# Second layer's output product by Strassen's scheme, as a phase of its own, and one written order for the first layer

## The chip, the cores and the metric

The kernel runs on one core of one Trainium2 chip. The metric is the device time of one execution in microseconds (us), lower is better. One execution was also profiled; rows below are from that one.

## What is computed

Three stages follow each other (reference, cut):

```python
# q, k, v: (4, 8, 576, 64), phi: (4, 8, 576, 32)
a = softmax(phi, axis=seq)                    # pools 576 keys into 32
k_m, v_m = a.T @ k, a.T @ v                   # per batch and head
x = softmax(q @ k_m.T / 8) @ v_m              # -> x: (2304, 512)
h = max(x @ w1, x @ w2, x @ w3)               # first layer, 512 -> 768
y = h @ w_out                                 # 768 -> 512
h2 = y @ w_in                                 # second layer, 512 -> 2048
g = max(h2, 0) + log1p(exp(-abs(h2)))         # softplus
out = g @ w_out2                              # 2048 -> 512
```

The feed-forward weights arrive as 64-bit floats, seen as pairs of 32-bit words. Products of large matrices are made in three fp32r matmuls from split operands: each operand is written as a high part (rounded to fp32r) plus the rest, and hi*hi, lo*hi and hi*lo are added up in PSUM.

## The kernel before, in words

*First layer.* Attention runs in 8 units (batch b, group g of four heads). A list PLAN, walked inside a manual schedule, gives the order of all five engines by steps: loads (ph, ld, q, wl), pooling (mx, ex, ax, tr), transposes of q (qT), scores and softmax (sc, s0, s1, s2, fin), weight conversion (ca, c7, wo), the products U = v_m * w (u, u6), x * w as U times attention (m1), splits of h (hs) and y = h * w_out (mo, ev). PLAN covers the first half of the tokens (1152 of 2304). The second half is done after it by phase_a (L743: m1 for six column blocks j, with conversions and U of later blocks put in by slots) and phase_o (L772: m1out and the evictions y_out, L717). There the order on each engine is left to the scheduler, which takes what its own timing model holds ready. y0_split (L853) splits the first half's y into y0h and y0l, one of twelve pieces in each of slots 4 to 15 of phase_a.

*Second layer.* The 2048 inner columns f come in 16 blocks of 128, four at a time (fg), the tokens in 6 chunks ck of 384: 96 steps (fg, ck, fi). In a step, m2in (L878) makes h2 for a block and chunk with 12 matmuls of 384 columns (4 blocks of dm x 3 split products) into one of two pst banks. soft1 (L894) takes |h| on VectorE (L896), softplus(-|h|) on ScalarE (L898) and max(h, 0) + that on VectorE (L900). soft2 (L903) splits it: gh by a cast on ScalarE, gl by a subtraction on GpSimd (both by the helpers cast, L189, and rest, L197). m2out (L942) multiplies by the output weights: 3 token tiles x 3 split products, 9 matmuls of 512 columns into three acc banks that add up over the four fi. After each (fg, ck) the sums are added to O in SBUF (L974), after the last fg stored. m2out of a step is two steps behind its m2in. Two m2in steps are done inside phase_o.

*Weights of the second layer.* w2_load (L836) loads a block of w_in and w_out2 (512 KB each); Conv.a joins the two 32-bit words to fp32 (top on ScalarE, then L234, L235, L238 on VectorE), Conv.b casts on ScalarE and subtracts on GpSimd. w2_steps (L847) hangs load, a and b on step numbers.

Engines work in the order of their own queues. A tile pool gives each tag a fixed number of buffers (bufs); a new tile of the tag waits until all uses of an older one have ended. The second layer's order is the scheduler's, with program order as priority.

Of the kernel before, what the change touches and what calls it, by code (L numbers as in the profile page):

```python
# [111 lines left out]
@with_exitstack
def fused_kernel(ctx: ExitStack, tc: tile.TileContext, q, k, v, phi, w1, w2, w3, w_out, m_in, m_out, out):
# [318 lines left out]
    def att_q(u):  # L432
# [30 lines left out]
        for s in range(3):  # L463
            ev(s, qps[s])
            if s < 2:
                yield
# [559 lines left out]
```

## Time and profile before

| what | value |
|---|---|
| timed runs | 714.68, 714.69, 710.29 us; median 714.68 |
| profiled execution | 711.26 us, span 709.5 us, mean granted clock 0.987 |
| TensorE matmul busy | 672.6 us (95%) in 4216 matmuls |
| VectorE / ScalarE / GpSimd busy | 415.6 / 302.9 / 258.2 us |
| HBM read / written | 53.74 / 4.72 MB |

The span goes from the first to the last instruction; the 1.8 us between it and the profiled time lie around it. PE is the TensorE matmul, PEld its weight load, DVE VectorE, ACT ScalarE, POOL GpSimd, SP SyncE, which issues the DMAs. Matmuls overlap, so the duration of one is longer than its distance to the next: what a matmul costs is read from the chain (time of a row by its count).

### The profile page before, as it was taken

To read this page: it belongs to the slowest core of one execution; us is meant where nothing else is said; L and a number is where in the kernel's file an instruction comes from. 1 tells how busy PE (TensorE), PEld (TensorE's weight loads), DVE (VectorE), ACT (ScalarE), POOL (GpSimd) and SP (SyncE) were. 2 spreads that over 40 slices of the span, in tenths; PEclk is the share of its full clock that TensorE was granted. 3 is DMA by queue.
4 is the path that set the end of the run, shared out by engine and by line. 5 is a ranking of instruction groups with operands and counts; after the bars stand their busy time and mean duration, and the time that the engine had idled before them with its cause. 6 is when DMAs were issued, how large, how long until landed. Compare 5 with 4: busy or idle time off the path is not lost.

```text
span 709.5 us, 11378 instructions
## 1 busy us (share of the span) xinstructions
PE 672.6 (95%) x4216; PEld 602.5 (85%) x4216; DVE 415.6 (59%) x785; ACT 302.9 (43%) x644; POOL 258.2 (36%) x278
## 2 busy tenths in 40 slices
...
GB/s 228 273 287 122 269 270 132 221 30 90 60 140 100 1 1 149 118 90 1 1 0 1 106 131 1 1 0 33 117 89 1 1 1 0 1 46 45 45 45 89
DMA packets 57463, 59.19 MB, mean 83 GB/s; under 512 B 9792, under 2 KB 52288, under 8 KB 57408
## 3 DMA queue, kind: packets, MB, share of 16 engines
...
q14 instruction: 22, 0.18, 0.1%
HBM read 53.74 MB, written 4.72 MB: 82 GB/s over the span
## 4 chain that ended last, share of the span: by engine, by line
PE 76%; DMA 8%; DVE 7%; ACT 3%; issue 2%; POOL 2%; SPq 1%; DVEq 0%; ACTq 0%; POOLq 0%
PE acc L953 28%; PE pst L890 28%; PE psm L661 11%; DMA kvm<-in_v_dram 2%; PE psm L711 2%; PE psm L712 2%; PE psm L713 2%; DMA kvm<-in_k_dram 2%; SPq L166 1%; DVE cg L235 1%; PE psm L607 1%; DMA qr<-in_q_dram 1%; DMA qn<-in_q_dram 1%; POOL y0l L199 1%; DMA pre<-in_q_dram 1%
## 5 line engine op out<-in xcount | busy, mean ns | idle before, releaser
L199 POOL TENSOR_TENSOR gl<-m,gh 128x384 fp32r<-128x384 f32 x96 | 100.2, 1044 | 241.5 <-ACT gh L191 233.9
L896 DVE TENSOR_SCALAR e<-pst 128x384 int32<-128x384 int32 x96 | 53.4, 556 | 147.9 <-PE pst L890 147.9
L898 ACT ACTIVATE L<-e 128x384 f32<-128x384 f32 x96 | 50.3, 524 | 183.8 <-DVE e L896 183.8
L953 PE MATMUL acc<-ol,gh 128*128 128x512 f32 x288 | 113.4, 394 | 0.0
L953 PE MATMUL acc<-oh,gh 128*128 128x512 f32 x288 | 113.3, 394 | 0.0
L890 PE MATMUL pst<-yb,ih 128*128 128x384 f32 x384 | 106.2, 337 | 0.0
L661 PE MATMUL psm<-ah,uh 128*128 128x288 f32 x288 | 87.4, 305 | 5.1 <-ACT mt L668 3.1
L900 DVE SCALAR_TENSOR_TENSOR m<-pst,L 128x384 f32<-128x384 f32 x96 | 53.5, 557 | 59.7 <-ACT L L898 59.7
L661 PE MATMUL psm<-al,uh 128*128 128x288 f32 x288 | 85.0, 295 | 1.2 <-DVE al L199 1.2
L661 PE MATMUL psm<-ah,ul 128*128 128x288 f32 x288 | 84.8, 295 | 0.0
L953 PE MATMUL acc<-oh,gl 128*128 128x512 f32 x288 | 81.9, 392 | 0.0
L191 ACT ACTIVATE gh<-m 128x384 fp32r<-128x384 f32 x96 | 50.3, 524 | 57.7 <-DVE m L900 57.5
L890 PEld LDWEIGHTS pst<-yb,ih 128*128 128x128 f32 x384 | 70.2, 188 | 2.2
L890 PE MATMUL pst<-y0l,ih 128*128 128x384 f32 x192 | 64.8, 337 | 0.0
L953 PEld LDWEIGHTS acc<-oh,gl 128*128 128x128 f32 x288 | 54.1, 188 | 12.5
L890 PE MATMUL pst<-y0h,ih 128*128 128x384 f32 x192 | 64.6, 337 | 0.0
L890 PE MATMUL pst<-yb,il 128*128 128x384 f32 x192 | 64.5, 336 | 0.0
L890 PE MATMUL pst<-y0h,il 128*128 128x384 f32 x192 | 64.5, 336 | 0.0
L661 PEld LDWEIGHTS psm<-ah,uh 128*128 128x128 f32 x288 | 54.2, 189 | 9.3 <-ACT mt L668 4.1
L953 PEld LDWEIGHTS acc<-oh,gh 128*128 128x128 f32 x288 | 53.9, 187 | 8.8 <-DVE yb L199 0.2
L953 PEld LDWEIGHTS acc<-ol,gh 128*128 128x128 f32 x288 | 54.1, 188 | 8.3
L661 PEld LDWEIGHTS psm<-al,uh 128*128 128x128 f32 x288 | 54.2, 188 | 1.4 <-DVE al L199 1.4
...
## 6 DMA issues: line engine op xcount, KB each, us to landing
wraw<-in_moe_w_dram SPq DMA_DIRECT2D x66, 256.0 KB, 4.1
raw<-in_moe_w_in_dram SPq DMA_DIRECT2D x16, 512.0 KB, 3.6
raw<-in_moe_w_out_dram SPq DMA_DIRECT2D x16, 512.0 KB, 3.5
kvm<-in_k_dram SPq DMA_DIRECT2D x8, 512.0 KB, 6.6
kvm<-in_v_dram SPq DMA_DIRECT2D x8, 512.0 KB, 5.8
wor<-in_moe_w_out_dram SPq DMA_DIRECT2D x6, 512.0 KB, 3.7
ph<-in_phi_dram SPq DMA_DIRECT2D x8, 256.0 KB, 4.1
qn<-in_q_dram SPq DMA_DIRECT2D x4, 512.0 KB, 6.0
```

The costliest lines, as they stand in the source:

```text
L166: eng.dma_start(**kw)
L191: nc.scalar.activation(out=dst, in_=src, func=AF.Copy)
L199: return e.tensor_tensor(out=dst, in0=src, in1=hi, op=ALU.subtract)
L661: nc.tensor.matmul(x, l[:, t, ws], r[:, cs], start=(n == 0), stop=(n == 5))
L711: nc.tensor.matmul(x, wh[:, ds], hi, start=first, stop=False)
L712: nc.tensor.matmul(x, wl[:, ds], hi, start=False, stop=False)
L713: nc.tensor.matmul(x, wh[:, ds], lo, start=False, stop=last)
L890: i = nc.tensor.matmul(hx, l[:, ds], r[:, cs], start=(n == 0), stop=(n == 3 * ND - 1))
L896: nc.vector.tensor_scalar(out=e.bitcast(I32), in0=hx.bitcast(I32), scalar1=0x7FFFFFFF, scalar2=None, op0=ALU.bitwise_and)
L898: nc.scalar.activation(out=L, in_=e, func=AF.Softplus, scale=-1.0)
L900: nc.vector.scalar_tensor_tensor(out=m, in0=hx, scalar=0.0, in1=L, op0=ALU.max, op1=ALU.add)
L953: nc.tensor.matmul(acc[0][t], l[:, t * P:(t + 1) * P], r, **kw)
```

## The change

1. m2in, soft and the order (fg, ck, fi) of the 96 steps stay, but a step's softplus result isn't split and multiplied: it is written to DRAM (Gd) in m. FORD makes the blocks of both inner halves alternate, so that the first inner quarter of both halves is complete after two fg. PSUM for m2in: six psx banks.
2. After the 96 steps comes the output product by Strassen's scheme (in the form with 7 products and shared sums). The tokens' halves (tile t and t + 9), the inner halves and the halves of the 512 output columns make the 2 x 2 blocks. 18 units (t, kh) each load four 128x512 tiles (g_load), form sums and split seven operands (g_parts), and multiply (g_mm: 7 operands x 4 blocks j x 3 split products of 256 columns). After both kh of a tile, g_out combines the seven products and stores two tiles.
3. The output weights are loaded and joined by pairs (w2_raw, q_join), combined (q_sums) and split (q_parts), spread over the steps; the last two pairs after the loop. Their split parts for pairs 4 to 7 go into the memory of y0, ya and yb.
4. PLAN is new and covers the whole first layer, with all of its second half, the splits of y (y0, ev2), the conversion of the first four w_in blocks (w2c) and the first three m2in steps; phase_a and phase_o go. att_q evicts a transposed block before the third is made. The fence on DMAs after PLAN (LOADED) goes.

```diff
@@ second layer: one step
-        G[n] = m
-    def soft2(n):
-        m = G[n]
-        gh = s_p.tile([P, CH], F32R, tag="gh", name="gh", bufs=3)
-        gl = s_p.tile([P, CH], F32R, tag="gl", name="gl", bufs=3)
-        cast("act", gh, m)
-        rest("pool", gl, m, gh)
-        G[n] = (gh, gl)
+        m = late["s"].tile([P, CH], F32, tag="m", name="m", bufs=4)
+        nc.vector.scalar_tensor_tensor(out=m, in0=hx, scalar=0.0, in1=e, op0=ALU.max, op1=ALU.add)
+        yield
+        half, i = divmod(FORD[fg * FG + fi], NP)
+        kh, j = divmod(i, FG)
+        if (ck, half, kh) not in Gd:
+            Gd[ck, half, kh] = gd_p.tile([NTT, P, FG, P], F32, name=f"gd{ck}{half}{kh}")
+        dma(out=Gd[ck, half, kh][:, :, j].rearrange("t p c -> p t c"), in_=m.rearrange("p (t c) -> p t c", t=NTT))
...
+    def x_tile():
+        return g_p.tile([P, DM], F32, tag="x", name="x", bufs=6)
...
+    def q_sums(i):
+        g1, g2 = J[2 * i], J[2 * i + 1]
+        WQ[i] = wq_tiles(i)
+        ta, tb = TS[i] = [x_tile() for _ in range(2)]
+        t1, t2, t4, t3 = ta[:, 0:Q], ta[:, Q:], tb[:, 0:Q], tb[:, Q:]
+        e = nc.gpsimd if i < FG + 2 else nc.vector
+        e.tensor_tensor(out=t1, in0=g1[:, Q:], in1=g1[:, 0:Q], op=ALU.subtract)
+        e.tensor_tensor(out=t2, in0=g2[:, Q:], in1=t1, op=ALU.subtract)
+        e.tensor_tensor(out=t4, in0=t2, in1=g2[:, 0:Q], op=ALU.subtract)
+        e.tensor_tensor(out=t3, in0=g2[:, Q:], in1=g1[:, Q:], op=ALU.subtract)
+    def q_parts(i):
...
+        for k, (h, l, x) in enumerate(((h0[:, 0:Q], l0[:, 0:Q], g1[:, 0:Q]), (h0[:, Q:3 * Q], l0[:, Q:3 * Q], g2),
+                                       (h0[:, 3 * Q:], l0[:, 3 * Q:], ta[:, 0:Q]), (h1[:, 0:Q], l1[:, 0:Q], ta[:, Q:]),
+                                       (h1[:, Q:], l1[:, Q:], tb))):
+            cast("act", h, x)
+            rest("dve" if k == 4 and i >= FG + 2 else "pool", l, x, h)
...
+    for i in range(NP):
+        if i < FG:
+            q_steps(16 + 18 * i if i < 3 else 84, i, 2)
+        elif i < FG + 2:
+            q_steps(GS * (NG2 - 1) + 12 + 5 * (i - FG), i, 1)
+        else:
+            q_steps(GS * (NG2 - 1) + 1 + 5 * (i - FG - 2), i, 1)
+    OPS = ("11", "S2", "S3", "S1", "22", "S4", "12")
...
+    UN = [(0, 0), (1, 0), (0, 1), (1, 1)] + [(t, h) for t in range(2, NCH * NTT) for h in range(2)]
+    def g_load(n):
...
+        for o in ("21", "22", "11", "12"):
+            x[o] = x_tile()
+            ck, half = t // NTT + (NCH if o[0] == "2" else 0), int(o[1]) - 1
+            dma(out=x[o], in_=Gd[ck, half, kh][t % NTT].rearrange("p j c -> p (j c)"))
+    def g_parts(n):
...
+        def parts(*os):
+            for o in os:
+                k = OPS.index(o)
+                h, l = (g_tile(n % 2, y, k) for y in "hl")
+                cast("act", h, x[o])
+                rest("dve" if o in ("S1", "S4", "11") else "pool", l, x[o], h)
+                hl[o] = (h, l)
+        tt("S1", "21", "22", ALU.add)
+        x["S3"] = x.pop("21")
+        parts("22")
+        tt("S3", "11", "S3", ALU.subtract)
+        tt("S2", "S1", "11", ALU.subtract)
+        parts("11", "S1")
+        tt("S4", "12", "S2", ALU.subtract)
+        parts("S2", "S3", "12", "S4")
...
+    def g_mm(n):
...
+            for y, (a, b) in enumerate(((h, wh), (h, wl), (l, wh))):
+                nc.tensor.matmul(PX[t][o], a[:, c], b, start=(kh == 0 and j == 0 and y == 0 and OPS.index(o) % 2 == 0),
+                                 stop=(kh == 1 and j == FG - 1 and y == 2 and (OPS.index(o) % 2 == 1 or o == "12")))
+        for o, j in [(o, j) for j in range(FG) for o in OPS] if kh and t < 2 else [(o, j) for o in OPS for j in range(FG)]:
+            one(o, j)
+    def g_out(t):
...
+        cast("act", p1, p["11"])
+        tt(u, p1, p["S2"], ALU.add)
+        tt(o1[:, Q:], u, p["S1"])
+        tt(u, u, p["S3"])
+        tt(o2[:, Q:], u, p["S1"])
+        tt(o2[:, 0:Q], u, p["22"], ALU.subtract)
+        store(t + NCH * NTT, o2, 0, DM)
+        tt(o1[:, Q:], o1[:, Q:], p["S4"])
...
+        tt(o1[:, 0:Q], p1, p["12"])
+        store(t, o1, 0, Q if t == NCH * NTT - 1 else DM)
...
     for n in range(2, len(seq)):
+        go(soft(n, m2in(n) if n > 2 else G.pop("hx")))
         for fn in bg.get(n, ()):
             fn()
-        m2out(n - 2)
+        if n == GS * (NG2 - 1) + 20:
+            g_load(0)
+            g_parts(0)
+    for i in (FG + 2, FG + 3):
+        q_sums(i)
+        q_parts(i)
+    for n in range(len(UN)):
+        if n + 1 < len(UN):
+            g_load(n + 1)
+            g_parts(n + 1)
+        g_mm(n)
+        if UN[n][1]:
+            g_out(UN[n][0])
```

(P = 128, DM = 512, CH = 384, Q = 256, FG = 4, NG2 = 4, NP = 8, NCH = NTT = 3, GS = 24. In g_parts, tt is a tensor_tensor of two x tiles on VectorE. The other weights tiles of a pair and the loads of w_in keep Conv's operations.)

## Rows read from the trace of the kernel before

**Rows 1.** By stretch: length, busy us (instructions) PE, PEld, DVE, ACT, POOL; clock, DMA share, GB/s.
```profile
0.00:60.00 60.00, 40.52 (x533) 28.15 (x535) 40.74 (x98) 28.77 (x70) 19.51 (x45) 0.86 0.93 263
60.00:178.00 118.00, 115.37 (x932) 99.91 (x927) 92.28 (x204) 69.40 (x170) 56.05 (x70) 1.00 0.52 155
178.00:306.00 128.00, 118.68 (x764) 114.50 (x764) 99.63 (x175) 76.04 (x163) 59.09 (x51) 1.00 0.26 83
306.00:704.00 398.00, 398.00 (x1995) 359.94 (x1993) 181.44 (x308) 128.70 (x243) 123.55 (x114) 1.00 0.12 34
704.00:709.50 5.50, 0.04 (x1) 0.00 (x0) 1.51 (x3) 0.00 (x0) 0.00 (x0) 0.92 0.43 143
```

**Rows 2.** Waits of TensorE, 0 to 62 us: total us, times, longest.
```profile
PE pst L325 <- DVE mx L322: 9.0, 3, 5.2
```

**Rows 3.** Waits of TensorE, 178 to 300 us.
```profile
PE psm L711 <- DVE yb L199: 3.4, 2, 2.3
PE psm L661 <- ACT mt L668: 3.1, 2, 2.8
```

**Rows 4.** Chain of waits, over the whole span: start, us, what.
```profile
244.95 14.31 PE psm L661 x108
...
306.36 4.19 PE pst L890 x24
...
321.08 2.08 PE acc L953 x9
```

**Rows 5.** Timeline, 183 to 191 us: start, us, instruction, count [idle before].
```profile
183.86 5.08 ACT L191 ACTIVATE y0h<-ya 128x384 fp32r<-128x384 f32 x12
...
184.46 12.83 POOL L199 TENSOR_TENSOR y0l<-ya,y0h 128x384 fp32r<-128x384 f32 x12 [3.02 <-ACT y0h L191]
...
190.71 0.40 PE L661 MATMUL psm<-ah,uh 128*128 128x288 f32 x1 [2.80 <-ACT mt L668]
```

**Rows 6.** Timeline, VectorE and GpSimd, 270.8 to 275.3 us.
```profile
270.87 0.69 DVE L235 SCALAR_TENSOR_TENSOR cg<-raw,cg 128x512 int32<-128x512 int32 x1
...
272.20 0.42 DVE L234 TENSOR_SCALAR cg<-cg 128x512 int32<-128x512 int32 x1
...
272.42 1.07 POOL L199 TENSOR_TENSOR hlo<-h,hh 128x384 fp32r<-128x384 f32 x1 [2.52 <-ACT hh L191]
...
272.65 1.39 DVE L235 SCALAR_TENSOR_TENSOR cg<-raw,cg 128x512 int32<-128x512 int32 x1
...
273.46 1.73 POOL L199 TENSOR_TENSOR il<-cg,ih 128x512 fp32r<-128x512 f32 x1
```

**Rows 7.** Groups by line and shape: count, busy us, mean ns; GpSimd, ScalarE, VectorE.
```profile
L199 POOL TENSOR_TENSOR gl<-m,gh 128x384 fp32r<-128x384 f32 x96 | 100.2, 1044 | 241.5 <-ACT gh L191 233.9 <-issue 4.4 <-PE acc L953 3.1
...
L199 POOL TENSOR_TENSOR ol<-cg,oh 128x512 fp32r<-128x512 f32 x16 | 21.7, 1355 | 19.8 <-ACT oh L191 19.8
...
L199 POOL TENSOR_TENSOR wo<-cg,wo 128x256 fp32r<-128x256 f32 x12 | 9.2, 765 | 23.2 <-ACT wo L191 18.5 <-DVE wl L235 4.8
...
L191 ACT ACTIVATE oh<-cg 128x512 fp32r<-128x512 f32 x16 | 10.0, 627 | 11.6 <-DVE cg L238 8.7 <-PE acc L953 2.9
...
L900 DVE SCALAR_TENSOR_TENSOR m<-pst,L 128x384 f32<-128x384 f32 x96 | 53.5, 557 | 59.7 <-ACT L L898 59.7
...
L974 DVE TENSOR_TENSOR o<-o,acc 128x512 f32<-128x512 f32 x54 | 33.8, 679 | 3.9 <-PE acc L953 3.9
...
L671 DVE TENSOR_TENSOR h<-mt,psm 128x288 f32<-128x288 f32 x48 | 21.6, 451 | 5.3 <-PE psm L661 1.6 <-PE psm L607 0.5 <-PE psm L629 0.5
```

**Rows 8.** DMA issues: count, KB each, median us to landing.
```profile
raw<-in_moe_w_out_dram SPq DMA_DIRECT2D x16, 512.0 KB, 3.5
...
out_dram<-o SPq DMA_DIRECT2D x8, 128.0 KB, 2.4
out_dram<-o SPq DMA_DIRECT2D x3, 256.0 KB, 2.8
```

**Rows 9.** Timeline, the end, from 703 us.
```profile
703.63 1.88 DVE L974 TENSOR_TENSOR o<-o,acc 128x512 f32<-128x512 f32 x3 [3.87 <-PE acc L953]
```

More of the change, by code (lines that the diff above doesn't have):

```diff
@@ L106 @@
     'al': ['dve'] * 8,
-    'us1': 0,
     'aq': (0, 1),
@@ L457, in ev @@
                 cast("act", qT[:, 2 * s:2 * s + 2, 0:2 * P], qp.rearrange("p (h c) -> p h c", h=2))
-        qps = []
-        for s in range(3):
-            qps.append(pe(s))
-            yield
[L463 to L466, printed above, removed]
+        qps = [pe(0)]
+        yield
+        qps.append(pe(1))
+        yield
+        ev(0, qps[0])
+        yield
+        qps.append(pe(2))
+        yield
+        ev(1, qps[1])
+        yield
+        ev(2, qps[2])
         d["qT"] = qT
@@ L811, in fused_kernel @@
                  wo=wo_step, hs=lambda cc, j: hsplit(0, cc, j), mo=lambda cc, j: m1out(0, cc, j), ev=y_step)
-    gens, DONE = {}, set()
     order = {getattr(mybir.EngineType, x) for x in C["order"]}
-    with tc.manual_schedule(engines=order):
-        for st in PLAN:
-            if st[0] in LOADS:
-                LOADS[st[0]](*st[1:])
-                continue
-            if st not in gens:
-                gens[st] = STEPS[st[0]](*st[1:])
-            if next(gens[st], DONE) is DONE:
-                DONE.add(st)
-        for st, g in gens.items():
-            assert next(g, DONE) is DONE
-            DONE.add(st)
@@ L826, in fused_kernel, with walk @@
-    a2_s.close()
-    y0_p = pool(ctx, "y0", side="left")
-    c_p = pool(ctx, "cwork", side="left")
-    u_p = pool(a1_s, "u2", side="right")
+    def walk(plan, loads, steps):
+        gens, DONE = {}, set()
+        with tc.manual_schedule(engines=order):
+            for st in plan:
+                if st[0] in loads:
+                    loads[st[0]](*st[1:])
+                    continue
+                if st not in gens:
+                    gens[st] = steps[st[0]](*st[1:])
+                if next(gens[st], DONE) is DONE:
+                    DONE.add(st)
+            for st, g in gens.items():
+                assert st in DONE or next(g, DONE) is DONE, st
@@ L847, in w2_steps, with late_pools @@
-    def w2_steps(bg, s, f, gap=1, **kw):
-        bg[s].append(lambda: w2_load(f, **kw))
-        for x in range(2):
-            bg[s + gap * (1 + x)].append(lambda x=x: cv[f, x].a())
-            bg[s + gap * (1 + x) + 1].append(lambda x=x: cv[f, x].b())
-    def y0_split(dm, c):
+    NP = NF // 2
+    FORD = [x for i in range(NP) for x in (i, i + NP)]
+    y0, W2, cv, late = {}, {}, {}, {}
+    G = {}
+    gd_p = pool(ctx, "gd", space=bass.MemoryType.DRAM)
+    Gd = {}
+    def late_pools():
+        if not late:
+            a1_s.close()
+            late["y"] = pool(ctx, "y1b", side="left")
+            late["w"] = pool(ctx, "w2", side="left")
+            late["s"] = pool(ctx, "soft", side="left")
@@ new lines, in w2_tiles, with w2_conv, wc_step, tiles @@
+    def w2_tiles(f, x):
+        late_pools()
+        W2[f][0:2] = [late["w"].tile([P, DM], F32R, tag=t, name=t, bufs=FG + 2) for t in ("ih", "il")]
+        return W2[f][0:2]
+    def w2_conv(f, x):
+        c = cv[f, x] = Conv(W2[f][2 * x], DM, None, None, mid["c"], bufs=3, sgn="bits") if f > 1 else Conv(W2[f][2 * x], DM, None, None, mid["c"], bufs=3)
+        return late_conv(c, lambda: w2_tiles(f, x))
+    def wc_step(i, p):
+        def tiles():
+            wj_t[i, p] = w_hl()
+            return wj_t[i, p]
+        c = CK["w", i, p] = Conv(raw_t[i, p // 2][:, p % 2].rearrange("p w f t -> p (w f) t"), 3 * P, None, None, a_p)
+        return late_conv(c, tiles)
@@ L854, in y0_split, with late_conv, y0_step @@
+    def late_conv(c, tiles):
+        c.top()
+        yield
+        c.join()
+        c.done = False
+        yield
+        c.hi, c.lo = tiles()
+        cast("act", c.hi, c.g)
+        yield
+        rest("pool", c.lo, c.g, c.hi)
+        c.done = True
+    def y0_step(dm, c):
         y, cs = y1[0, dm], slice(c * CH, (c + 1) * CH)
         if c == 0:
-            y0[dm] = tuple(y0_p.tile([P, TOK], F32R, name=f"y0{x}{dm}") for x in "hl")
+            y0[dm] = tuple(mid_pool("y0").tile([P, TOK], F32R, name=f"y0{x}{dm}") for x in "hl")
@@ L925, in fused_kernel @@
+    def front(n):
+        hx = m2in(n)
+        if n == 2:
+            G["hx"] = hx
+            return
+        yield
+        yield from soft(n, hx)
+    walk(PLAN, dict(wl=w_load, w2l=w2_raw, **LOADS),
+         dict(c=wc_step, u1=u_mr, y0=y0_step, w2c=w2_conv, hs2=lambda cc, x: hsplit(1, cc, jof(NJ + x)),
+              mo2=lambda cc, x: m1out(1, cc, jof(NJ + x)), ev2=yb_step, **{"in": front}, **STEPS))
     right.close()
     psA_s.close()
-    b_p = pool(ctx, "bwork", side="right")
+    wq_p = pool(ctx, "wq", side="right")
@@ L928, in fused_kernel, with w2_load, w2_steps @@
+    g_p = pool(ctx, "g", side="right")
     psx = pool(ctx, "psx", space=PSUM)
+    Q = 2 * P
+    J, WQ, TS = {}, {}, {}
+    def x_tile():
+        return g_p.tile([P, DM], F32, tag="x", name="x", bufs=6)
+    def w2_load(f):
+        w2_raw(f, 0)
+        cv[f, 0] = Conv(W2[f][0], DM, None, None, mid["c"], bufs=3, sgn="bits")
+        cv[f, 0].hi, cv[f, 0].lo = w2_tiles(f, 0)
+    def w2_steps(bg, s, f, gap=1):
+        bg[s].append(lambda: w2_load(f))
+        bg[s + gap].append(lambda: cv[f, 0].a())
+        bg[s + gap + 1].append(lambda: cv[f, 0].b())
@@ new lines, in wq_tiles @@
+    def wq_tiles(i):
+        if i < FG:
+            return [[wq_p.tile([P, n * Q], F32R, name=f"q{x}{i}{n}") for n in (4, 3)] for x in "hl"]
+        if i < FG + 2:
+            k = 2 * (i - FG)
+            t = [mid["y0"].tile([P, TOK], F32R, tag=f"y0{x}{dm}", name=f"q{x}{i}{dm}") for x in "hl" for dm in (k, k + 1)]
+        else:
+            k = 2 * (i - FG - 2)
+            t = [pl.tile([P, TOK], F32R, tag=f"{g}{dm}", name=f"q{g}{i}{dm}") for pl, g in ((y1a_p, "ya"), (late["y"], "yb"))
+                 for dm in (k, k + 1)]
+        t = [x[:, 0:(4 - n % 2) * Q] for n, x in enumerate(t)]
+        return [t[0:2], t[2:4]]
@@ new lines, in q_join @@
+    def q_join(x):
+        i, half = divmod(x, 2)
+        if i < FG + 2:
+            g = mid["c"].tile([P, DM], F32, tag="cg", name="cg", bufs=3)
+        else:
+            g = late["w"].tile([P, DM], F32R, tag=("ih", "il")[half], name="qj", bufs=FG + 2).bitcast(F32)
+        c = Conv(W2[x][2], DM, None, None, mid["c"], sgn="bits", g=g)
+        c.a()
+        J[x] = g
+    def q_sums(i):
[8 more added lines that the diff above has]
+        e.tensor_tensor(out=t3, in0=g2[:, Q:], in1=g1[:, Q:], op=ALU.subtract)
@@ new lines, in g_mm, with one @@
+    def g_mm(n):
+        t, kh = UN[n]
+        x = GU[n]
+        if kh == 0:
+            ps = [psx.tile([P, 512], F32, tag="x", name="psx", bufs=6) if k < 2 or t % 2 == 0 else pst() for k in range(4)]
+            PX[t] = {o: ps[k // 2][:, k % 2 * Q:(k % 2 + 1) * Q] for k, o in enumerate(("11", "S2", "S3", "S1", "22", "S4", "12"))}
+        def one(o, j):
+            h, l = x[o]
+            w, k = WOF[o]
+            wh, wl = (y[w][:, k * Q:(k + 1) * Q] for y in WQ[FG * kh + j])
+            c = slice(j * P, (j + 1) * P)
+            for y, (a, b) in enumerate(((h, wh), (h, wl), (l, wh))):
[3 more added lines that the diff above has]
+            one(o, j)
```

276 lines of the change are left out of this document (100 added, 176 removed), and 211 rows, old and new, of the table PLAN.

## The prediction

> **What bounds the kernel now.** I began with the busy time by stretch, since the page's 95% busy TensorE is a mean over stages. From 306 to 704 us TensorE is busy without a break at the full clock (granted 1.00, the 2.4 GHz level): this is the second layer, 56% of the span [rows 1]. VectorE is busy there for 181 of 398 us, ScalarE for 129, GpSimd for 124, the DMA engines at 12%. So in that stretch only a shorter TensorE stream helps, and the other engines have room. The 31.4 us in which TensorE idles in the first layer lie mostly in two places: 19.5 us before 60 us, where the DMA engines are 93% busy, and 9.3 us between 178 and 306 us [rows 1]. The table of waits then says for what it waited: at the start 9.0 us for the maxima on VectorE [rows 2], later 3.4 us for the yb splits and 3.1 us for the mt copies [rows 3]. Last, the chain of waits: from 306 us it is nothing but TensorE, alternating 2.10 us for 12 matmuls of 384 columns (m2in; the first row has two, 4.19 for 24) and 2.08 us for 9 of 512 (m2out) [rows 4]. The chain ends in 5.5 us without matmuls: three additions of 0.68 us and the last stores [rows 1, 9].
>
> **The output product's matmuls.** Before: 96 steps of 9 matmuls of 512 columns, 864 x 0.2311 us (2.08 / 9) = 199.7 us [rows 4]. After: 18 units (9 token tiles, two inner halves), each with 7 operands x 4 inner blocks x 3 split products = 84 matmuls of 256 columns, 1512 in all: 7/8 of the columns in 1.75 times as many instructions. No split matmul of 256 columns stands in the trace, so I take a line through two rows of the chain: 288 columns take 14.31 / 108 = 0.1325 us, 512 take 0.2311, which is 0.00044 us a column and gives 0.1184 us at 256. The same line gives 0.1747 at 384, which is the row's 4.19 / 24. Thus a unit takes 84 x 0.1184 = 9.95 us and the phase 179.0 us: **20.7 us less**. The upper bound is that 256 columns cost as much as 288 (200.3 us, nothing gained). For the lower one I use 0.0004167 us a column, the 2.4 GHz clock that the rows show as granted, with no cost per matmul: 161.3 us. I take the line, because it meets three sizes.
>
> The Trainium skill's "TensorE: Matmul & The Clock Gate", section "Back-to-back issue gap", gives an isolated gap of N/2.4 + 2.5 ns. It would make 256 columns 0.109 us and the phase 165 us; at 288 it says 0.1225 where the row has 0.1325, so here the trace decides.
>
> **The first product and softplus.** The 12 matmuls a step stay: 96 x 2.10 us. Each step loses its split (gh on ScalarE, gl on GpSimd) and gains a 196 KB write to DRAM, one in 2.10 us, or 94 GB/s. Weight loads (28 of 512 KB in some 195 us) add 75 GB/s; the DMA engines have carried 263 GB/s in a stretch [rows 1], so I cost the writes at nothing. If that cover were gone, four m buffers give 8 us before VectorE would block. VectorE has two PSUM operations a step, 2 x 0.557 = 1.11 of 2.10 us, plus 28 weight conversions of 0.42 + 0.69 + 0.69 us: 157 of 195 us. It fits, with six PSUM buffers as slack. The fourfold faster turn of weight groups (50 us instead of 100) leaves the last two conversions of a group about 10 us from issue to use, against 3.5 us of load and about 5 of work [rows 7, 8]: 0 to 2 us, taken as 0.
>
> **Preparing the operands.** Each unit loads four 256 KB tiles from DRAM and makes seven operands. VectorE has four sums and three splits with both inputs in SBUF, GpSimd four splits, ScalarE seven casts of 0.63 us (4.4 us). At 512 columns such an operation takes VectorE 0.69 and GpSimd 1.36 us [rows 6, 7]. They can't be laid side by side: the VectorE operation L235, 0.69 us alone at 270.87, took 1.39 us from 272.65, while a GpSimd subtraction ran until 273.49, and ended 0.55 us after it; the next GpSimd subtraction, issued at 273.46, took 1.73 us and ended 1.15 us after VectorE's [rows 6]. Operations that read PSUM keep their time. So each unit needs 7 x 0.55 + 4 x 1.15 = 8.45 us in which the two exclude each other, within 9.95 us of matmuls: it just fits. The combination of a token tile (seven additions from PSUM, 0.42 us each by the line through 0.451 at 288 and 0.679 at 512 columns [rows 7]) adds 1.5 us of VectorE a unit, outside that exclusion.
>
> The Trainium skill's "SBUF — State Buffer", section "Who interferes with whom", has the rule: VectorE with two SBUF inputs and GpSimd share a port, whoever starts first has it for the whole instruction, and the other blocks. Taken literally (whole durations) it makes the phase port-bound, the second rival below; the rows show some 0.14 us of each operation overlapping.
>
> **The start of the phase** has no such room, and this is the cost I expect. The weight splits of pairs 6 and 7 go into yb's memory, so they wait for the last m2in. Their exclusive time is 2 x (3 x 0.62 + 1.15 + 0.55) = 7.1 us (0.765 us at 256 columns [rows 7] less 0.14 is 0.62), and until then they hold four of the six x buffers. Unit 1's loads land about 3.5 us later, between the 2.8 and 3.5 us of such transfers [rows 8]: 10.6 us after the loop. Its preparation takes 8.45 us plus handoffs, say 10, so it ends at 20.6, where its last operand is wanted at 18.5. Unit 2 multiplies block by block over all seven operands, so all must be ready; they are at about 30.6 and were wanted at 19.9. From unit 3 on, preparation and matmuls have the same 10 us. With about 1 us at unit 0 (pairs 3 to 5 are split in the last 25 us of the loop) this is **12 us given back**, between 0 (all made earlier) and 24 (one more whole preparation exposed).
>
> **The first layer's order.** Program order was hoisted here: the twelve y0 casts, written to slots 4 to 15 of phase_a, ran in one row from 183.86 us, and TensorE waited 2.80 us behind them for an mt copy [rows 5]. A written order can take such waits away. Of the 9.3 us between 178 and 306 I take 6; the start is bound by DMA and its loads are only permuted, so 0 there. **6 us less**, between 31 less (every idle moment gone) and 10 more (two stalls like the 5.2 us one [rows 2]). Two more m2in steps move into this stretch; same work, 0.
>
> **The end.** Before, 5.5 us after the last matmul [rows 1]. After, one addition of 0.42 us and a store of half a tile, about 2.4 us [rows 8]: **2 us less**.
>
> Sum, against the profiled execution's 711.3 us (span 709.5 and 1.8 around it, which stay): 711.3 - 20.7 + 12 - 6 - 2 = 694.6, forecast 695 us. The median of the three runs, 714.7, is 3.4 above the profiled execution and the lowest 1.0 below; I stay on the profiled one.
>
> **Rivals.**
> - *No stall at the start*: weights converted ahead. For it: GpSimd is busy 124 of 398 us [rows 1] and loses 100 us of gl, so there is time earlier. Against: the memory of y0 and yb isn't free earlier. 711.3 - 20.7 - 6 - 2 = 682.6 us.
> - *The shared port bounds every unit* (slower): if the exclusion covers whole durations, 7 x 0.69 + 4 x 1.36 + 1.5 = 11.8 us a unit, 211.8 us for 18 against 199.7. 711.3 + 12.1 + 12 - 8 = 727 us. It decides from 10.9 us a unit (18 x 10.9 = 199.7 - 12 + 8). For it: the 1.39 and 1.73 us rows. Against: the 0.55 and 1.15 us remainders in them.
> - *The new order loses in the first layer*: 8 us more instead of 6 less, 709 us. The first 60 us are full of fine dependencies [rows 2], for it; that later waits are few and named, against.
> - *Fewer columns bring nothing*: 256 columns cost like 288. 711.3 + 0.6 + 12 - 8 = 716 us. Against: the line meets 288, 384 and 512.
>
> **How the numbers follow.** Forecast 0.52 (its own range 686 to 704), no stall 0.18, port-bound 0.10, order loses 0.13, no gain from columns 0.07. About 1% (7 us) is what a measurement of this kernel can tell from no change. Faster by over 1% (below 704): 0.52 x 0.95 + 0.18 + 0.13 x 0.3 = 0.71, as 0.72. Slower by over 1% (above 718): port-bound and some of the last, 0.11. Within: 0.17. The range for 8 in 10 reaches down to the first rival and up to the last, 682 to 714.
>
> **What would show it.** Right: chain rows of about 0.118 us a matmul in the new phase, units near 10 us from the fourth on, waits of TensorE for splits of together about 12 us in the first three units, two-input VectorE operations stretched by GpSimd. Wrong: units of 11 us or more throughout (port), gaps inside the m2in loop (conversions or DRAM writes late), 0.13 us a matmul, or a second layer that starts later than 306 us.

## The result, and the profile after

| | before | after |
|---|---|---|
| runs beside each other, median | 713.64 us (710.29 to 714.69) | 702.78 us (698.08 to 704.15) |
| ratio, 95% interval | | 0.9842 [0.9805, 0.9878] |
| profiled execution / span | 711.26 / 709.5 us | 701.71 / 699.9 us |

The change makes the kernel 1.6% faster; the forecast was 695 us, 8 us less than measured. First the busy time of the changed kernel by stretch, with the columns of [rows 1]; the stretches from 400 us on are its own (end of the m2in loop at 497, first three units, the other fifteen, the end):

```profile
178.00:306.00 128.00, 122.38 (x788) 120.20 (x788) 92.78 (x173) 71.72 (x155) 52.72 (x50) 0.99 0.29 87
306.00:400.00 94.00, 94.00 (x545) 94.00 (x543) 68.13 (x118) 36.26 (x69) 21.97 (x20) 1.00 0.48 138
400.00:497.00 97.00, 96.71 (x558) 96.39 (x557) 72.98 (x130) 40.11 (x79) 37.65 (x37) 1.00 0.58 168
497.00:545.00 48.00, 37.64 (x268) 36.56 (x269) 41.81 (x46) 22.24 (x41) 34.85 (x24) 0.86 0.37 115
545.00:695.00 150.00, 149.62 (x1247) 149.22 (x1245) 122.86 (x159) 57.60 (x107) 86.87 (x56) 1.00 0.40 120
695.00:699.90 4.90, 0.00 (x0) 0.00 (x0) 0.68 (x3) 0.00 (x0) 0.00 (x0) 0.72 0.38 107
```

The m2in loop has no gap, with the DMA engines at 48 to 58%. The last fifteen units have none either: 149.62 us for 1247 recorded matmuls, 0.120 us each. Only the stretch from 497 to 545 us is broken: TensorE is busy for 37.64 of 48 us, at a mean granted clock of 0.86. The timeline of TensorE shows the five gaps there (start, us, instruction, idle before it):

```profile
498.44 0.38 PE L1092 MATMUL psx<-qh,gh 128*128 128x256 f32 x1 [1.73 <-ACT gh L239]
500.29 0.58 PE L1092 MATMUL psx<-qh,gh 128*128 128x256 f32 x1 [1.35 <-ACT gh L239]
517.46 0.58 PE L1092 MATMUL pst<-qh,gh 128*128 128x256 f32 x1 [4.36 <-ACT gh L239]
518.87 0.58 PE L1092 MATMUL psx<-qh,gh 128*128 128x256 f32 x1 [0.62 <-ACT gh L239]
534.47 0.39 PE L1092 MATMUL psx<-qh,gh 128*128 128x256 f32 x1 [2.58 <-ACT gh L239]
```

The first two are unit 0's, the next two unit 1's, the last is within unit 2. All name ScalarE's cast, but a cast waits for its sum: ahead of it stand VectorE and GpSimd. Their timeline in that stretch (pieces):

```profile
499.50 5.20 POOL L247 TENSOR_TENSOR gl<-x,gh 128x512 fp32r<-128x512 f32 x3 [0.47 <-ACT gh L239]
500.57 2.99 DVE L247 TENSOR_TENSOR gl<-x,gh 128x512 fp32r<-128x512 f32 x2
503.48 1.77 DVE L1060 TENSOR_TENSOR x<-x 128x512 f32<-128x512 f32 x1
504.66 4.94 POOL L247 TENSOR_TENSOR qyb<-qj,qya 128x256 fp32r<-128x256 f32 x4
512.16 0.55 DVE L915 SCALAR_TENSOR_TENSOR m<-psx,e 128x384 f32<-128x384 f32 x1
513.97 0.41 DVE L986 TENSOR_TENSOR x<-x,qj 128x256 f32<-128x256 f32 x1
515.08 0.69 DVE L247 TENSOR_TENSOR qyb<-x,qya 128x512 fp32r<-128x512 f32 x1 [0.70 <-ACT qya L239]
516.88 0.69 DVE L1060 TENSOR_TENSOR x<-x 128x512 f32<-128x512 f32 x1 [1.10 <-DMA x<-gd]
```

Unit 0's splits (gl), the sums and splits of pairs 6 and 7 (L984 to L987, qyb) and the last softplus results (m) follow each other until 515.8 us. A 512-column operation that takes 0.69 us alone takes 1.77 beside GpSimd; the loop's last m comes at 512.16, 15 us after the loop's last matmul. Unit 1's first sum starts at 516.88. SyncE's timeline shows why not earlier: unit 1's four loads stand behind five writes of m, and the waits of SyncE's queue from 495 to 516 us are for m (16.1 us).

```profile
495.02 18.07 SPq L214 DMA_DIRECT2D gd<-m  x5
513.18 1.87 SPq L214 DMA_DIRECT2D x<-gd  x4
```

The clock by stretch, around the first two waits:

```profile
499.00:506.00 7.00, 5.71 (x27) 5.71 (x28) 7.00 (x8) 4.45 (x10) 6.53 (x6) 0.51 0.10 30
506.00:516.00 10.00, 7.09 (x57) 6.71 (x56) 9.07 (x15) 3.68 (x8) 7.29 (x7) 1.00 0.37 106
516.00:523.00 7.00, 4.92 (x21) 4.63 (x22) 5.40 (x6) 3.45 (x6) 4.33 (x3) 0.51 0.34 120
```

From 499 to 506 and from 516 to 523 us the granted clock is at half (0.51, the 1.2 GHz level). The first time it fell in the wait of 1.35 us that came right behind the one of 1.73, the second time in the wait of 4.36 us. Matmuls follow each other there at 0.21 us; some 50 of them at 0.21 in place of 0.12 cost 4.7 us. The 2.58 us wait at 534 us brought no such spell.

In the first layer the waits of TensorE between 178 and 300 us that answer to [rows 3] are these (total us, times, longest); the 2.8 us wait for mt is gone:

```profile
PE psm L702 <- DVE ul L684: 1.9, 4, 0.8
PE psm L752 <- DVE yb L247: 0.7, 1, 0.7
```

The fourth m2in step started at 308.30 us before, and starts at 301.68 now. The first line is the kernel before, the second the changed one:

```profile
308.30 0.33 PE L890 MATMUL pst<-y0h,ih 128*128 128x384 f32 x1
301.68 0.69 PE L903 MATMUL psx<-y0h,ih 128*128 128x384 f32 x1 [2.55 <-DVE yb L247]
```

The second line shows one more wait, just behind the 300 us. With it the waits for yb come to 3.3 us, where they were 3.4 before [rows 3]: they stayed. TensorE's idle time between 178 and 306 us fell from 9.3 [rows 1] to 5.6 us and hardly changed ahead of that (21.9 for 22.1), so it accounts for 4 of the 6.6 us; where the rest comes from stays open. In and behind that wait the granted clock was at half, from 301.2 to 304.6 us, which takes in the first 3 us of the loop:

```profile
299.00:305.00 6.00, 3.45 (x12) 3.32 (x12) 2.59 (x6) 2.87 (x7) 5.73 (x7) 0.72 0.30 92
```

The account, span against span (before's last matmul ended at 704.0, after's at 694.6 us):

| term | predicted | measured |
|---|---|---|
| columns | -20.7 | -18.4 (18 units of 10.07 us, 181.3, for 199.7) |
| start of the phase | +12 | +16.7 (496.7 to 694.6 is 197.9; less 181.2) |
| first layer | -6 | -6.6 (301.7 for 308.3) |
| end | -2 | -0.2 (5.3 for 5.5) |
| m2in loop | 0 | -1.0 (93 steps: 195.0 for 395.7 - 199.7) |
| sum | -16.7 | -9.5 (the spans differ by 9.6) |

The loop's 195.0 us include its first 3 us at half clock. The same loop took 193.7 us in x5 and x8 below, whose profiles have no half clock there.

### The profile page after: what moved, and what is told of

Same layout as the page of the kernel before. It is cut to its first block, busy times and chain, and to the rows that moved or that the text cites. A ratio compares the mean times of both kernels' runs of the same rounds, so it can differ in the third digit from the quotient of the medians.

```text
span 699.9 us, 13357 instructions
## 1 busy us (share of the span) xinstructions
PE 656.5 (94%) x4864; PEld 626.8 (90%) x4864; DVE 539.3 (77%) x926; ACT 329.6 (47%) x695; POOL 314.3 (45%) x300
## 5 line engine op out<-in xcount | busy, mean ns | idle before, releaser
L247 POOL TENSOR_TENSOR gl<-x,gh 128x512 fp32r<-128x512 f32 x72 | 113.1, 1597 | 68.7 <-ACT gh L239 65.3
L239 ACT ACTIVATE gh<-x 128x512 fp32r<-128x512 f32 x126 | 72.3, 623 | 106.0 <-DMA x<-gd 53.5
L903 PE MATMUL psx<-yb,ih 128*128 128x384 f32 x384 | 98.0, 334 | 0.0
L1092 PE MATMUL psx<-qh,gh 128*128 128x256 f32 x306 | 88.4, 289 | 6.3 <-ACT gh L239 6.3
L1092 PE MATMUL psx<-qh,gl 128*128 128x256 f32 x306 | 87.4, 288 | 0.0
L1092 PE MATMUL psx<-ql,gh 128*128 128x256 f32 x306 | 87.4, 287 | 0.0
L1060 DVE TENSOR_TENSOR x<-x 128x512 f32<-128x512 f32 x72 | 69.7, 989 | 16.8 <-DMA x<-gd 14.6
L247 DVE TENSOR_TENSOR gl<-x,gh 128x512 fp32r<-128x512 f32 x54 | 67.6, 1264 | 14.6 <-ACT gh L239 14.5
L915 DVE SCALAR_TENSOR_TENSOR m<-psx,e 128x384 f32<-128x384 f32 x93 | 51.4, 554 | 31.8 <-ACT e L912 31.8
L247 POOL TENSOR_TENSOR il<-cg,ih 128x512 fp32r<-128x512 f32 x16 | 21.9, 1368 | 115.6 <-ACT ih L239 86.4
L903 PEld LDWEIGHTS psx<-yb,ih 128*128 128x128 f32 x384 | 69.3, 188 | 0.0
L903 PE MATMUL psx<-yb,il 128*128 128x384 f32 x192 | 64.1, 334 | 0.0
```

The costliest lines, as they stand in the source:

```text
L239: nc.scalar.activation(out=dst, in_=src, func=AF.Copy)
L247: return e.tensor_tensor(out=dst, in0=src, in1=hi, op=ALU.subtract)
L903: nc.tensor.matmul(hx, l[:, ds], r[:, cs], start=(k == 0), stop=(k == 3 * ND - 1))
L915: nc.vector.scalar_tensor_tensor(out=m, in0=hx, scalar=0.0, in1=e, op0=ALU.max, op1=ALU.add)
L1060: nc.vector.tensor_tensor(out=x[o], in0=x[a], in1=x[b], op=op)
L1092: nc.tensor.matmul(PX[t][o], a[:, c], b, start=(kh == 0 and j == 0 and y == 0 and OPS.index(o) % 2 == 0), stop=(kh == 1 and j == FG - 1 an ...
```

## The experiments

Each is the changed kernel with one edit, unless it says otherwise. The first layer is the same in all, yet their profiles show the fourth m2in step anywhere from 299.3 to 304.6 us; so the phase is compared by distances from the end of the loop's last matmul. The kernel before was timed again beside each group of runs (medians from 711.4 to 713.6 us), so ratios compare better than medians. The table has them, from the traces, in us: first matmul of units 1, 2 and 3, and "start cost", the time from the loop's end to the phase's last matmul less 181.2 us. Without any stall it would be 10.1, 20.1, 30.2 and 0.

| kernel | unit 1 | unit 2 | unit 3 | start cost | median, us | ratio to before, 95% interval |
|---|---|---|---|---|---|---|
| changed kernel | 20.8 | 33.7 | 46.5 | 16.7 | 702.8 | 0.984 [0.981, 0.988] |
| x1 unit 0 early | 10.2 | 26.3 | 37.1 | 7.0 | 696.8 | 0.979 [0.974, 0.984] |
| x2 pairs late | 16.1 | 31.1 | 46.9 | 16.8 | 701.9 | 0.986 [0.981, 0.990] |
| x3 sums in raw | 19.7 | 31.8 | 43.2 | 13.2 | 703.4 | 0.988 [0.985, 0.991] |
| x4 no GpSimd splits | 18.1 | 28.2 | 38.1 | 8.0 | 693.0 | 0.973 [0.969, 0.976] |
| x8 fill | 22.2 | 37.4 | 47.3 | 17.3 | 702.0 | 0.987 [0.980, 0.993] |
| x6 all early | 9.9 | 21.9 | 31.8 | 1.8 | 689.7 | 0.968 [0.965, 0.971] |

### What makes the start: port work, x buffers, or order?

**x1**, unit 0's preparation written at step 64 in place of 92:

```diff
-        if n == GS * (NG2 - 1) + 20:
+        if n == GS * (NG2 - 1) - 8:
             g_load(0)
```

> Unit 0's loads, sums and splits are written 28 steps earlier, in step 64 of the loop, where VectorE and GpSimd have room; nothing else changes. In the changed kernel GpSimd ran unit 0's last splits from 499.5 to 504.7 us and the sums and splits of pairs 6 and 7 followed until 515.8 us. Theory A (the port work of VectorE and GpSimd queued at the loop's end sets the start): pairs 6 and 7 begin some 5 us earlier, unit 1 with them, and the time falls by 4 to 7 us, to 696 to 699. Rival B (the x buffers and the load that follows set it, whatever was queued before): below 2 us. Rival C (unit 0 was needed that late anyway, and its work only moves into m2in steps that then wait): the m2in loop gets gaps, no gain or a loss.

The start cost fell from 16.7 to 7.0 us, the span by 8.3 (2.0 of it an earlier first layer, within the spread named above). But the loop got 4.3 us longer (199.3 us for 93 steps): TensorE waited 2.2 us for m at 414 to 416 us, and behind that the clock was at half from 417.1 to 420.6 us. So A holds, with a part of C. The median fell by 6 us; the intervals of the two ratios still overlap.

**x2**, pairs 6 and 7 behind unit 1's preparation:

```diff
-    for i in (FG + 2, FG + 3):
-        q_sums(i)
-        q_parts(i)
     for n in range(len(UN)):
...
             g_parts(n + 1)
+        if n == 0:
+            for i in (FG + 2, FG + 3):
+                q_sums(i)
+                q_parts(i)
```

> The sums and splits of pairs 6 and 7 are written behind unit 1's loads and splits in place of ahead of them. They are first used in unit 2. Theory A (port work): the sum of work ahead of unit 2 is the same, so unit 1's wait of 4.4 us goes and unit 2's grows; only the 3 us in which both engines stood waiting for unit 1's loads can be won: 0 to 4 us, 699 to 703. Theory B (x buffers held by pairs 6 and 7): the loads of units 1 and 2 start at the loop's end, and most of the 12 to 16 us of the start goes: 690 to 694.

SyncE's timeline has unit 1's loads at 505.06 us, 5.2 us after this kernel's loop end (499.9), where the changed kernel issued them 16.5 us after its own:

```profile
505.06 4.22 SPq L214 DMA_DIRECT2D x<-gd  x4
```

Unit 1 came 4.7 us sooner, and unit 3 as late as before. The wait moved, as theory A says; nothing was won.

**x3**, buffers for pairs 6 and 7 that hold no x buffer:

```diff
-        ta, tb = TS[i] = [x_tile() for _ in range(2)]
+        if i < FG + 2:
+            ta, tb = TS[i] = [x_tile() for _ in range(2)]
+        else:
+            r = mid["c"].tile([P, DM, 2], I32, tag="r", name="ts", bufs=2).bitcast(F32).rearrange("p a b -> p (a b)")
+            ta, tb = TS[i] = [r[:, 0:DM], r[:, DM:]]
```

> The four sums of pairs 6 and 7 are kept in the free tiles of the raw weights in place of x buffers, so that unit 1's four loads no longer wait for these pairs. Theory B (the x buffers set the start): unit 1's loads start when the loop ends, about 500 us in place of 513 to 515, unit 1 begins without its 4.4 us wait: 5 us or more won, 697 or less. Theory A (port work, and SyncE's queue, where these loads stand behind writes that wait for VectorE until 512.7 us): the loads start at most 1 to 2 us earlier, 701 to 703.

Unit 1's loads were issued 7.1 us after the loop's end (509.71 for 502.6), 9.4 us sooner than in the changed kernel: no longer tied to these buffers, they stand ahead of the last write of m in SyncE's queue. Yet 3.5 us of start cost is all that went, and the scheduler, no longer bound by the buffers, did these sums ahead of unit 0's work, so that they ran from 487 to 500 us on VectorE and TensorE waited 2.6 us for m within the loop, which took 198.8 us in place of 195.0. No gain in sum: theory B falls. (Theory A had the time about right, 701 to 703, but not the loads, which it let start 1 to 2 us earlier.)

**x4**, without GpSimd's splits (the low parts of four of seven operands are left out):

```diff
-                rest("dve" if o in ("S1", "S4", "11") else "pool", l, x[o], h)
+                if o in ("S1", "S4", "11"):
+                    rest("dve", l, x[o], h)
+                else:
+                    l = h
```

> The four splits a unit on GpSimd are left out (the high part stands where the low part is multiplied), all matmuls, casts, loads and VectorE work stay; the low parts of four of the seven operands are left out of the result. Theory A (VectorE and GpSimd exclude each other): 4.6 us of exclusive time a unit goes, so units 1 and 2 are ready some 5 and 9 us earlier and the time falls by 8 to 12 us, to 691 to 695, while units from the fourth on stay at 10.07 us, since there the matmuls set the pace. Rival (buffers and loads set the start): less than 3 us. If the splits also cost the later units something, these fall below 10.0 us, towards 9.95.

693.0 us, within A's 691 to 695. The groups of the steady stretch (553 to 690 us) give the reason. Changed kernel, then x4 (count, busy us, mean ns):

```profile
L247 POOL TENSOR_TENSOR gl<-x,gh 128x512 fp32r<-128x512 f32 x53 | 81.8, 1570 | 55.0 <-ACT gh L239 51.6 <-PE psx L1092 3.5
L1060 DVE TENSOR_TENSOR x<-x 128x512 f32<-128x512 f32 x52 | 49.8, 979 | 11.9 <-DMA x<-gd 9.8 <-POOL gl L247 1.4
L247 DVE TENSOR_TENSOR gl<-x,gh 128x512 fp32r<-128x512 f32 x39 | 49.8, 1285 | 12.3 <-ACT gh L239 12.3
```

```profile
L1060 DVE TENSOR_TENSOR x<-x 128x512 f32<-128x512 f32 x48 | 32.9, 690 | 15.4 <-DMA x<-gd 7.9 <-ACT gh L239 6.4
L247 DVE TENSOR_TENSOR gl<-x,gh 128x512 fp32r<-128x512 f32 x36 | 24.5, 689 | 26.1 <-ACT gh L239 25.9
```

Without GpSimd, VectorE's operations fall from 979 and 1285 ns to 690. The later units stay at 10.07 us: there the matmuls set the pace. This edit takes GpSimd's own time out of the start as well as the exclusion; x5 tells the two apart.

**x5**, GpSimd's splits done twice from unit 4 on:

```diff
+                if n > 3 and o in ("22", "S2", "S3", "12"):
+                    rest("pool", l, x[o], h)
                 hl[o] = (h, l)
```

> From unit 4 on, each of GpSimd's four splits a unit is done twice (same values). Theory A (VectorE's two-input operations and GpSimd's exclude each other but for some 0.14 us each): a unit needs 7 x 0.55 + 8 x 1.15 = 13.05 us in which they exclude each other, so units 4 to 17 take 13.0 us in place of 10.07, 14 x 2.98 = 42 us more: about 744. Rival (they run beside each other): GpSimd alone needs 8 x 1.28 to 1.36 = 10.2 to 10.9 us a unit, 14 x 0.2 to 0.8 = 2 to 11 us more: 705 to 714.

746.5 us (ratio 1.048 [1.043, 1.054]): theory A, to 2.5 us. Units 4 to 17 took 13.20 us each in the trace; forecast 13.0. By stretch:

```profile
553.00:738.00 185.00, 157.04 (x1181) 150.07 (x1181) 132.84 (x142) 57.79 (x99) 164.45 (x109) 0.95 0.32 96
```

and GpSimd's splits in it:

```profile
L247 POOL TENSOR_TENSOR gl<-x,gh 128x512 fp32r<-128x512 f32 x109 | 164.9, 1549 | 18.0 <-ACT gh L239 18.0
```

GpSimd is busy for 164 of 185 us, since its operations are stretched too (109 of them in 164.9 us, 1.55 us each, where one that VectorE did not hold up took 1.28 at 497.75 us of the changed kernel). The price of 0.55 and 1.15 us, read from two overlaps of the old trace [rows 6], thus carries over. By the Trainium skill's "SBUF — State Buffer", section "Who interferes with whom", one that holds the shared port has it for the whole instruction; with whole durations a unit would be 7 x 0.69 + 8 x 1.28 = 15.1 us. The run shows 13.2 us, so about 0.12 us of each of the 15 operations overlaps.

**x8**, 36 matmuls into an unused half bank ahead of unit 1:

```diff
+            if n == 0:
+                PX["d"] = ps[3][:, Q:]
...
+        if n == 1:
+            h = GU[0]["12"][0]
+            for _ in range(36):
+                nc.tensor.matmul(PX["d"], h[:, 0:P], WQ[0][0][0][:, 0:Q], start=False, stop=False)
```

> 36 matmuls of 256 columns (4.3 us) into an unused half bank stand ahead of unit 1, where TensorE waited 4.36 us and then ran at half clock from 516.2 to 523.0 us. Nothing else changes. Theory A (the idle stretch itself brings the half clock, and it is a cost beside the wait): unit 1 starts when it did, but at the full clock, its first matmuls take 0.12 us in place of 0.21, and some 2.2 us are won: about 700.5. Rival (the half clock comes from something else, or the next wait for unit 2 takes up what is won, since the port work ahead of unit 2 is the same): the profile shows full clock in unit 1 but unit 2 starts as late as before, no gain; or the half clock stays.

The idle time before unit 1 shrank to 0.94 us. But after two matmuls the same unit waited 3.03 us for a split, and in this wait, from 521.0 us, the clock fell to half again, until 527.8 us:

```profile
519.84 0.38 PE L1094 MATMUL psx<-qh,gh 128*128 128x256 f32 x1 [0.94 <-ACT gh L239]
523.37 0.58 PE L1094 MATMUL psx<-qh,gl 128*128 128x256 f32 x1 [3.03 <-DVE gl L247]
```

```profile
517.00:520.00 3.00, 2.06 (x17) 1.85 (x17) 1.58 (x3) 1.48 (x3) 0.79 (x1) 1.00 0.77 248
520.00:524.00 4.00, 0.97 (x5) 0.77 (x6) 4.00 (x5) 1.97 (x4) 2.23 (x3) 0.63 0.00 0
524.00:530.00 6.00, 6.00 (x38) 6.00 (x38) 4.89 (x5) 2.94 (x6) 4.11 (x3) 0.68 0.53 179
```

So unit 1 still had a long wait, and what it would take at the full clock isn't shown. Unit 3 began 47.3 us after the loop, no sooner: the rival holds. A wait filled with other matmuls wins nothing while the operands come no sooner.

### What the scheme itself brings

**x9**, the same kernel with a plain product (four splits a unit, 48 matmuls of 512 columns; the core of the edit):

```diff
-    OPS = ("11", "S2", "S3", "S1", "22", "S4", "12")
...
+    OPS = ("11", "12", "21", "22")
...
+        for k, o in enumerate(OPS):
+            h, l = (g_tile(n % 2, y, k) for y in "hl")
+            cast("act", h, x[o])
+            rest("dve" if k % 2 else "pool", l, x[o], h)
```

> Strassen's scheme alone is undone: the same first layer, the same m2in loop, DRAM writes and phase of its own with 18 units, but each unit splits its four operands and multiplies by 512 columns (48 matmuls a unit, no sums of operands or weights, the two products of a tile copied out). The phase's matmuls are 18 x 48 x 0.2311 = 199.7 us as before the change, against 181.2 us (18 x 10.07) with the scheme. Port work a unit: 2 x 0.55 + 2 x 1.15 = 3.4 us, so the start costs 1 to 3 us. Theory (first layer 6.6 us earlier, the phase of its own nearly free, the scheme's gain mostly eaten by its start): 711.3 - 6.6 + 1 to 3 = 706 to 708, some 5 us under the kernel before and 3 to 6 over the changed one. Rival (the way through DRAM or the phase costs by itself): at or above the kernel before. Rival (the scheme brings less than its columns): at or below the changed kernel.

698.7 us, ratio 0.9798 [0.9761, 0.9835]: lower than forecast by 8, and not above the changed kernel. The chain of waits ends in one row for the whole phase:

```profile
299.28 187.19 PE psx L903 x1068
486.51 8.59 PE psx L903 x48
495.10 196.99 PE psx L1060 x864
```

No start cost at all, and 196.99 / 864 = 0.228 us a matmul where the alternating order of before had 0.2311 [rows 4]; why is not settled. The profiled phase with the scheme took 197.9 us from the loop's end. So in the changed kernel the seven eighths of the columns were worth nothing in sum: its 16.7 us of start gave all of it back. Span against span, x9 is 13.1 us below the kernel before: 9.0 in the first layer, 2.7 in the output product's matmuls, 1.2 at the end. So the gain is that of the first layer's new order and of the undivided phases, as far as two traces can tell. Of the 3.6 us between the spans of x9 and of the changed kernel, 2.4 are an earlier first layer (299.3 for 301.7 us, the same code, within the spread named above) and 1.0 an end of 4.3 for 5.3 us.

### A faster version

**x7**, the last tile's outputs in x buffers, alone:

```diff
-            g_p.tile([P, DM], F32, tag=f"o{x}", name=f"o{x}", bufs=1) for x in range(2)]
+            g_p.tile([P, DM], F32, tag=f"o{x}", name=f"o{x}", bufs=1) if t < NCH * NTT - 1 else x_tile() for x in range(2)]
```

> The last token tile's two output buffers are taken from the x buffers, which are free by then, in place of the single o buffers, whose last stores held VectorE's final additions until 693.36 us. Theory (that wait set the end): after the last matmul there remain one addition of 0.4 to 0.5 us, the issue of six stores and their landing, 3.5 to 4 us in place of 5.3: 1.3 to 1.8 us less. Rival (the stores' own issue and landing set it): 0.

3.9 us after the last matmul, 1.4 less, as the theory had it. The median was 698.6 us, ratio 0.981 [0.977, 0.986]; what it has beyond 1.4 us is not this edit's (its profile has the first layer 1.7 us earlier, within the spread named above, and the same start cost, 16.9). Nor is it shown that the 1.4 us are: x4 and x6 keep the single o buffers, and their ends take 3.96 and 3.93 us, without that wait. Those of x1 and x8 take 4.5 and 4.3, with it. How much the wait costs thus depends on when the stores of the tile before go out. The chain of waits of the changed kernel shows the wait: a store's landing holds VectorE's additions.

```profile
691.14 2.10 DMA out_dram<-o
...
693.36 0.43 DVE o L1101
```

**x6**, what can be made ahead:

```diff
-            q_steps(16 + 18 * i if i < 3 else 84, i, 2)
+            q_steps(16 + 18 * i if i < 3 else 62, i, 2)
...
+    for i in (FG + 2, FG + 3):
+        bg[GS * (NG2 - 1) + 21 + i - FG - 2].append(lambda i=i: q_sums(i))
...
-        if n == GS * (NG2 - 1) + 20:
+        if n == GS * (NG2 - 1) + 8:
...
     for i in (FG + 2, FG + 3):
-        q_sums(i)
         q_parts(i)
```

(and x3's buffers)

> What can be made ahead is: unit 0's loads and splits are written at step 80, pair 3 at step 62 in place of 84, and the sums of pairs 6 and 7 at steps 93 and 94, into the free raw tiles; only their splits, which overwrite yb, stay behind the loop. Theory A (port work behind the loop's end sets the start): against the kernel with unit 0 early, 8 sums of 0.62 us more leave the start, and the 2.3 us gap that unit 0's work made in the loop at 413 us goes: start cost 3 to 5 us in place of 7.0, time 688 to 692. Rival (the last 15 steps of the loop are now as crowded as the start was): softplus results come late and the loop gets gaps, 695 to 700.

689.7 us, 3.2% [2.9, 3.5] under the kernel before and the lowest median of all: start cost 1.8 us, and units 0 to 2 at the full clock. The time is theory A's, but not by its terms: the start cost is below its 3 to 5 us, and the gap in the loop grew in place of going. The plain product (x9) lies 9 us higher (ratios 0.968 [0.965, 0.971] and 0.980 [0.976, 0.984]): with its operands made early, the scheme does pay. What is left is in the loop, which took 200.05 us in place of 195.0. Its busy time by stretch (the loop from 306 to 500, the first three units, the rest), and TensorE's waits from 306 to 540 us:

```profile
306.00:400.00 94.00, 94.00 (x544) 94.00 (x543) 68.19 (x118) 34.59 (x67) 22.95 (x22) 1.00 0.51 144
400.00:500.00 100.00, 95.81 (x542) 95.18 (x541) 86.58 (x145) 44.56 (x87) 45.18 (x41) 0.98 0.58 171
500.00:533.00 33.00, 31.37 (x260) 30.96 (x260) 28.56 (x31) 17.40 (x34) 27.11 (x19) 1.00 0.43 126
533.00:684.00 151.00, 150.99 (x1261) 150.78 (x1259) 121.27 (x158) 57.09 (x106) 86.81 (x56) 1.00 0.40 120
```

```profile
PE psx L903 <- DVE m L915: 4.2, 2, 3.3
PE psx L1099 <- POOL gl L247: 1.6, 2, 1.1
```

The 4.2 us are at 421 to 428 us, about step 60: unit 0's work, written at step 80, ran there as soon as its loads allowed, beside weight conversions, and held m on VectorE. Behind these waits the clock was at half from 428.9 to 432.3 us.

Three more runs were to remove that, all with x6's edits and x7's tail. **x10** holds unit 0's loads behind the write of step 74 (GATE); **x11** behind step 58, with unit 0 wholly on GpSimd; **x12** behind step 58 on both engines, with pair 3 back at step 84. What they share:

```diff
-            dma(out=x[o], in_=Gd[ck, half, kh][t % NTT].rearrange("p j c -> p (j c)"))
+            with tc.issue_after(MW[GATE if n == 0 else 2].ins):
+                dma(out=x[o], in_=Gd[ck, half, kh][t % NTT].rearrange("p j c -> p (j c)"))
```

> As the kernel with everything early, but unit 0's loads are held behind the DRAM write of step 74, since its work, written at step 80, was issued at step 57 to 61 and held softplus results on VectorE, so that the loop stood 4.9 us at 421 to 428 us; and with the last token tile's outputs in x buffers. Theory: the gaps in the loop go, the start stays at about 2 us, the tail at 3.9: 689.7 - 4.9 = 685, between 683 and 687. Rival (that work has no room in the loop wherever it is put, with three pairs of weights in the last 24 steps): gaps of the same size later in the loop, 688 to 691.

> As the kernel with everything early and the tail in x buffers, but all of unit 0's sums and splits (3 sums at least inside the loop, 7 splits) are on GpSimd, with its loads held behind the DRAM write of step 58, where GpSimd stood idle for 18 us. Theory (the gaps in the loop come from bursts of two-input work on VectorE that alternates with GpSimd's, 1.2 to 1.8 us each, ahead of the softplus operations): with VectorE free of unit 0 the loop's gaps shrink from 4.6 to 4.9 us to below 2 us, time 685 to 687. Rival (VectorE's weight conversions are held up by GpSimd all the same): gaps of 3 to 5 us, 688 to 691.

> The same with unit 0's work on both engines, its loads behind the write of step 58, and pair 3 back at step 84, so that the stretch from step 60 to 68 has unit 0 alone. Theory (it is the meeting of pair 3's and unit 0's work that made the gap at 421 to 428 us): gaps below 2 us, 685 to 687, if the last 12 steps take pair 3 as they did in the changed kernel. Rival (the last steps have room for pair 3 only as long as the sums of pairs 6 and 7 aren't there): gaps after step 84 or a start of 5 us and more, 689 to 693.

All three theories fell: 691.6, 692.2 and 696.8 us (ratios 0.970, 0.973 and 0.978), each above its rival's range too, by 0.6, 1.2 and 3.8 us. The loop took 199.6, 200.0 and 200.4 us, with TensorE's waits for m at other places: 3.6 us in x10, the longest at 470 us (1.9), 2.8 in x11, at 490 and 496 us, and 4.5 in x12, at 491 (2.6) and 499. The rest is shorter pauses and, in x11 and x12, 3.4 us at half clock. x12 also kept 6.6 us of start cost. So the work that was moved ahead costs some 5 us in the loop in all four orders that were tried; which order of VectorE's queue would hide it, or whether any does, stays open.

## Why the prediction came out as it did

*Direction and range right, the size 8 us off.* Step by step:

- **Columns, -20.7: a little too much.** 10.07 us a unit, 0.1199 a matmul, where the line through 288 and 512 columns gave 0.1184. That is 2.3 us. The rival "256 columns cost like 288" (0.1325) is out. The isolated gap in the Trainium skill's "TensorE: Matmul & The Clock Gate", section "Back-to-back issue gap", makes it 0.109, an estimate; the units here don't agree with that.
- **Start, +12: the mechanism right, one cost missing.** Of the 16.7 us, 4.7 are the half clock that came with the waits; the other 12.0 are the forecast number (the five waits shown, 10.6, and short pauses). That it is met so closely is luck: the forecast had about 1 us at unit 0 and most of the rest at unit 2, and the waits were 3.1 us in unit 0, 5.0 in unit 1 and 2.6 in unit 2. Unit 0's splits still ran until 504.7 us, and the eight sums of pairs 6 and 7, which VectorE made between 505.6 and 514.4 us, are in none of its terms. No term stood for the clock, though the stalls of the first 60 us of the old trace lie in a stretch with a mean clock of 0.86 [rows 1]. The working of the 12 had a part that fell: that pairs 6 and 7 hold x buffers and the loads land late. x2 and x3 had the loads out 11 and 9 us sooner and won nothing in sum. The other part, the exclusive time of VectorE and GpSimd, is shown by x1, x4 and x5.
- **First layer, -6: the number right, its working in part.** Of the 6.6 us, 4 are idle time of TensorE that went; the named mt wait is gone, the waits for yb stayed (3.3 for 3.4 us). Not tested by a run of its own: it is the distance between two traces, and the same code moved by up to 5 us between runs, though all thirteen profiles with the new order start the fourth m2in step 3.7 to 9.0 us sooner than the one of before.
- **End, -2: missed** (-0.2). The sum counted one addition and one store, but the single o buffers made VectorE wait for a store's landing first. Where that wait is missing (x4, x6, x7), the end takes 3.9 to 4.0 us, 1.5 less than before.
- **DRAM writes and conversions at 0: right.** From its fourth step on the loop has no gap.
- **The port as a rival, 727 us: not met**, and how near it is x5 shows: a unit of 13.2 us as soon as GpSimd has four operations more.
- **"No stall at the start", 682.6 us:** x6 removed all but 1.8 us of the stall and came to 689.7, mainly since the loop then grew by 5 us.

The weak point is the price of the start: x9 shows that in the changed kernel the saved columns were paid back whole by the scheme's own operands, and x6 that most of this price can be moved.
